# Attention kept transposed, column-tiled outputs and integer rounding in a fused attention and MLP kernel

## Chip, cores, metric

One core of one Trainium2 chip. The metric is the device time of one execution in microseconds (us), the median of several executions.

## The reference

```python
# q, k, v: (8, 8, 576, 64) float32;  g_norm: (64,)
# w_in: (512, 2048), w_out: (2048, 512): float64 (a float32 array times a NumPy scalar)
kv  = einsum('bhsd,bhse->bhde', k, v)
out = einsum('bhsd,bhde->bhse', q, kv)
rms = sqrt(mean(out * out, axis=-1, keepdims=True) + 1e-06)
x   = (out / rms * g_norm)            # -> (8*576, 8*64) = (4608, 512)
h   = x @ w_in
y   = maximum(0.01 * h, h) @ w_out    # (4608, 512) float32
```

The attention is linear: no softmax, only an RMS norm per head and token. The MLP has nine blocks of 512 tokens.

## The kernel before

A batch has 576 tokens: four tiles of 128 fill one MLP block, and the eight rests of 64 make a ninth. All matmuls are float32. TensorE turns q (transposes through PSUM), computes o token by token row, and turns the normalised x back.

```python
def load_batch(b):                       # q, k and v alike: 64 partitions in each transfer
    ...
    nc.sync.dma_start(t[:64], src[b, :, :SLO, :]...)
    nc.sync.dma_start(t[64:, :, :J], src[b, :, SLO:, :]...)

def round_f64(dst, src):                 # one tile of weights, 128 x 512
    nc.sync.dma_start(raw..., src.bitcast(U32))          # one transfer, 128 partitions
    nc.scalar.activation(low, lo, func=AF.Copy, scale=2.0 ** -52)
    nc.vector.tensor_scalar(mag, hi, 0x7FFFFFFF, None, op0=ALU.bitwise_and)
    nc.gpsimd.tensor_scalar(mag..., F64_MOST, F64_LEAST, op0=ALU.min, op1=ALU.max)
    ...                                  # three VectorE operations
    nc.gpsimd.tensor_mul(low, low, tmp.bitcast(F32))
    nc.gpsimd.tensor_add(low, low, mag.bitcast(F32))
    nc.vector.scalar_tensor_tensor(dst.bitcast(U32), in0=hi, scalar=0x80000000, in1=low..., ...)

def attend(parts):
    for h in range(H):                   # 64 columns of output a matmul
        nc.tensor.matmul(o_ps[part, h, :], lhsT=qT[:, h, :], rhs=kv[:, h, :], ...)
    ...

def mlp(b, xT, between):
    for f in range(NF + 1):              # NF = 16 chunks of 128 of the 2048
        ...                              # four matmuls into h_ps
        nc.scalar.activation(leak, h_ps, func=AF.Copy, scale=SLOPE)
        nc.vector.tensor_max(gT, h_ps, leak)
        ...                              # four matmuls of chunk f-1 into o_acc
        between(f)                       # rounding and attention steps are put here
    for t in range(4):
        nc.scalar.copy(o_sb, accs[t])    # three o_sb buffers
        store(b, t, o_sb)                # issued from ScalarE's queue

for b in range(B):
    if b == 0: go(w_steps, FC)           # twelve weight tiles before the first block
    def between(f):
        go(w_steps, 2)
        if b == 0 and f == 4: load_batch(1)
        if b > 0 or f > 7: go(a_steps, 1)
```

## Time and profile before

| | before |
|---|---|
| time, median | 1268.38 us (1267.89 to 1270.82) |
| profiled span | 1265.1 us |
| busy: TensorE / VectorE / ScalarE / GpSimd | 1203.1 / 259.5 / 223.1 / 107.3 us |
| block 0 of the MLP ends (with what comes before it: "start-up") | 243.75 us, two batches of attention done |
| later | TensorE never idle |

How to read the views: a *windows* row gives a stretch of time, its length, the busy time (and number of records) of TensorE, its weight loads, VectorE, ScalarE and GpSimd, then TensorE's granted clock, the DMA engines' share and GB/s. A *timeline* row gives start, duration, engine, source line, operation, output<-input, and in brackets the idle time before it and what ended that; a row at the edge of the window asked for is cut there, so its count can be short. "SPq" and "ACTq" are the queues that issue transfers. The rows of before stand in the prediction below. One view of before that the prediction does not show is its list of transfers (KB each, median us from issue to landing):

```profile
raw<-in_moe_w_in_dram SPq DMA_DIRECT2D x16, 512.0 KB, 3.6
```

A tile of w_in came as one transfer over 128 partitions, 3.6 us from issue to landing.

### The profile page before, as it was taken

Reading aid. Unit: us, or ns where it says so; the run is one execution under the profiler, and the core shown is the slowest. Engines: PE = TensorE matmul, PEld = TensorE weight load, DVE = VectorE, ACT = ScalarE, POOL = GpSimd, SP = SyncE. Lnnn points to the kernel's source line nnn. Section 1 sums busy time; section 2 is a strip of 40 time slices with the busy share of each in tenths; the row PEclk is TensorE's granted clock in tenths of the full one; section 3 lists DMA queues with packets and bytes.
Section 4 is the critical chain, followed back from the end, with each engine's and each line's share of the span. In section 5 each row is a group of like instructions: output and inputs, shape, how many; then the busy total and the mean of one; then the engine's idle time right before and its main releaser. Section 6 shows DMA issues by size and latency. Waiting matters only on the chain.

```text
span 1265.1 us, 9654 instructions
## 1 busy us (share of the span) xinstructions
PE 1203.1 (95%) x4048; PEld 605.6 (48%) x4048; DVE 259.5 (21%) x421; ACT 223.1 (18%) x402; POOL 107.3 (8%) x102
## 2 busy tenths in 40 slices
PE   5788579999999999999999999999999999999997
PEld 4533245465445544554455545544455444444443
DVE  0655765111001211121012100211011101011010
ACT  1411123212011310221012201220122110001001
POOL 0455654000000000000000000000000000000000
PEclk9998789999999999999999999999999999999999
DMA  8454261241014100501031101400100010001001
GB/s 181 123 153 120 96 170 47 53 75 38 0 25 83 38 1 1 100 10 37 0 71 37 38 1 34 75 1 0 34 1 1 1 30 4 1 0 34 1 0 33
DMA packets 35915, 55.14 MB, mean 44 GB/s; under 512 B 2592, under 2 KB 27168, under 8 KB 35872
## 3 DMA queue, kind: packets, MB, share of 16 engines
q1 hardware_dynamic: 29952, 45.09, 15.7%
q10 hardware_dynamic: 5920, 9.44, 3.3%
q8 instruction: 31, 0.51, 0.2%
q14 instruction: 12, 0.10, 0.0%
HBM read 45.09 MB, written 9.44 MB: 43 GB/s over the span
## 4 chain that ended last, share of the span: by engine, by line
PE 87%; DVE 5%; POOL 4%; issue 1%; DMA 1%; ACT 1%; ACTq 0%; SPq 0%; POOLq 0%; DVEq 0%
PE h_ps L252 36%; PE o_acc L265 36%; PE o_ps L183 6%; PE kv_ps L157 4%; PE q_ps L174 3%; POOL low L119 2%; POOL low L120 2%; DVE w L121 1%; DVE tmp L114 1%; PE x_ps L201 1%; POOL mag L111 1%; DMA v_in<-in_v_dram 1%; DVE mag L116 1%; DVE tmp L118 1%; DVE mag L110 1%
## 5 line engine op out<-in xcount | busy, mean ns | idle before, releaser
L265 PE MATMUL o_acc<-w,gT 128*128 128x512 f32 x1152 | 524.9, 600 | 13.7 <-DVE gT L258 13.7
L252 PE MATMUL h_ps<-xT,w 128*128 128x512 f32 x1024 | 472.4, 600 | 8.6 <-DVE w L121 7.8
L265 PEld LDWEIGHTS o_acc<-w,gT 128*128 128x128 f32 x1152 | 221.5, 193 | 296.6 <-issue 276.7
L252 PEld LDWEIGHTS h_ps<-xT,w 128*128 128x128 f32 x1024 | 189.3, 192 | 217.5 <-issue 204.7
L258 DVE TENSOR_TENSOR gT<-h_ps,leak 128x512 f32<-128x512 f32 x144 | 99.5, 691 | 692.0 <-ACT leak L256 692.0
L256 ACT ACTIVATE leak<-h_ps 128x512 f32<-128x512 f32 x144 | 85.8, 596 | 572.0 <-PE h_ps L252 572.0
L157 PE MATMUL kv_ps<-v_in,k_in 128*64 128x64 f32 (+1 forms) x640 | 60.5, 243 | 15.7 <-DMA v_in<-in_v_dram 15.7
L183 PEld LDWEIGHTS o_ps<-kv,qT 64*128 64x128 f32 x512 | 65.9, 205 | 17.8 <-issue 12.4
L183 PE MATMUL o_ps<-kv,qT 64*128 64x64 f32 x512 | 70.6, 293 | 3.2 <-DVE y L194 2.2
L157 PEld LDWEIGHTS kv_ps<-v_in,k_in 128*64 128x64 f32 (+1 forms) x640 | 50.5, 146 | 29.8 <-issue 21.0
L174 PE MATMUL q_ps<-ident,q_in 128*64 128x128 f32 (+1 forms) x320 | 49.9, 283 | 10.7 <-ACT qT L175 9.7
L252 PE MATMUL h_ps<-xT_rem,w 128*128 128x512 f32 x128 | 57.4, 592 | 0.0
L175 ACT COPY qT<-q_ps 64x512 f32<-64x512 f32 x64 | 36.9, 577 | 98.9 <-PE q_ps L174 97.1
L188 DVE TENSOR_REDUCE ss<-sq 128x8 f32<-128x512 f32 x36 | 24.7, 685 | 144.5 <-ACT sq L186 144.5
L174 PEld LDWEIGHTS q_ps<-ident,q_in 128*64 128x64 f32 (+1 forms) x320 | 30.2, 119 | 38.5 <-ACT qT L175 25.2
L119 POOL TENSOR_TENSOR low<-low,tmp 128x512 f32<-128x512 f32 x32 | 43.0, 1344 | 51.1 <-DVE tmp L118 49.5
L120 POOL TENSOR_TENSOR low<-low,mag 128x512 f32<-128x512 f32 x32 | 41.8, 1306 | 1.9
L186 ACT ACTIVATE sq<-o_ps 128x512 f32<-128x512 f32 x36 | 21.5, 597 | 113.9 <-PE o_ps L183 113.9
L252 PEld LDWEIGHTS h_ps<-xT_rem,w 128*128 128x128 f32 x128 | 24.3, 190 | 30.6 <-issue 30.6
L108 ACT ACTIVATE low<-raw 128x512 f32<-128x512 uint32 x32 | 21.7, 678 | 95.0 <-DVE w L121 84.9
L121 DVE SCALAR_TENSOR_TENSOR w<-raw,low 128x512 uint32<-128x512 uint32 x32 | 26.4, 826 | 40.2 <-POOL low L120 40.2
L202 ACT ACTIVATE xT<-x_ps,g_sb 128x512 f32<-128x512 f32 x32 | 21.2, 685 | 66.5 <-PE x_ps L201 66.5
(25 smaller groups left out, 240.3 us busy)
## 6 DMA issues: line engine op xcount, KB each, us to landing
out_dram<-o_sb ACTq DMA_DIRECT2D x72, 128.0 KB, 2.4
raw<-in_moe_w_in_dram SPq DMA_DIRECT2D x16, 512.0 KB, 3.6
raw<-in_moe_w_out_dram SPq DMA_DIRECT2D x16, 512.0 KB, 3.5
k_in<-in_k_dram SPq DMA_DIRECT2D x8, 640.0 KB, 6.1
v_in<-in_v_dram SPq DMA_DIRECT2D x8, 640.0 KB, 10.5
q_in<-in_q_dram SPq DMA_DIRECT2D x8, 640.0 KB, 6.4
k_in<-in_k_dram SPq DMA_DIRECT2D x8, 512.0 KB, 8.0
v_in<-in_v_dram SPq DMA_DIRECT2D x8, 512.0 KB, 12.3
```

The lines of the kernel that those rows point to most:

```text
L119: nc.gpsimd.tensor_mul(low, low, tmp.bitcast(F32))
L120: nc.gpsimd.tensor_add(low, low, mag.bitcast(F32))
L121: nc.vector.scalar_tensor_tensor(dst.bitcast(U32), in0=hi, scalar=0x80000000, in1=low.bitcast(U32), op0=ALU.bitwise_and, op1=ALU.bitwise_or)
L157: nc.tensor.matmul(kv_ps[:D, h, :], lhsT=k_in[:n, h, j, :], rhs=v_in[:n, h, j, :], start=(j == 0), stop=(j == JJ - 1))
L174: nc.tensor.transpose(tp[:D, h, :n], q_in[:n, h0 + h, j, :], ident[:n, :n])
L175: nc.scalar.copy(qT[:, h0:h0 + 4, :], tp[:D, :, :n])
L183: nc.tensor.matmul(o_ps[part, h, :], lhsT=qT[:, h, :], rhs=kv[:, h, :], start=True, stop=True)
L188: nc.vector.tensor_reduce(ss, sq, axis=AX.X, op=ALU.add)
L252: nc.tensor.matmul(h_ps, lhsT=w1_sb[f // FC][:, kk, (f % FC) * P:(f % FC + 1) * P], rhs=xT[:, kk, :], start=(kk == 0), stop=(kk == NK - 1))
L256: nc.scalar.activation(leak, h_ps, func=AF.Copy, scale=SLOPE)
L258: nc.vector.tensor_max(gT, h_ps, leak)
L265: nc.tensor.matmul(accs[t], lhsT=g_last[:, t * P:(t + 1) * P], rhs=w2_sb[c // FC][:, c % FC, :], start=(c == 0), stop=(c == NF - 1))
```

## The change

The intent: take transposes and narrow outputs off TensorE, and GpSimd out of the rounding.

- q is loaded in a layout that VectorE's 32x32 block transpose turns into [d, head, token]; k and v go to TensorE two heads side by side.
- o comes out transposed, [column of x, token]: for each of four groups of 128 columns of x, four matmuls of 32 weight columns each write one quarter of the PSUM partitions. x then needs no turning; the sums over a head are one matmul with a block matrix of ones.
- Tokens go straight through: block i is tokens 512i to 512i+511, so x tiles straddle batches.
- Leaky ReLU is one ScalarE pass; output copies move to VectorE.
- float64 is rounded by shifts and one integer addition on VectorE, with two ScalarE passes.

The source is not the order of the program: a scheduler in the framework orders each engine's instructions when the kernel is built. In the changed kernel it puts batch 1's attention, but for the last step, ahead of the first o_acc and batch 2's into block 0, whatever `f > 4` says.

```diff
+    def load_q(b):
+        q_in = ins.tile([P, NP, T * D], F32, tag="q_in", name="q_in", bufs=1)
+        for l in range(2):
+            for c in range(2):
+                r0, n = 64 * l + 32 * c, T * D - 32 * c
+                src = q[b].rearrange("(p l) (t s) d -> l t p (s d)", l=2, s=T)[l]
+                nc.sync.dma_start(q_in[r0:r0 + 32, :, :n], src[:, :, 32 * c:])
...
+        rows = P // len(srcs)                       # w_in: eight pieces of 16 partitions
+        for i, src in enumerate(srcs):
+            nc.sync.dma_start(raw[i * rows:(i + 1) * rows]..., src.bitcast(U32))
+        nc.scalar.activation(add, lo, func=AF.Copy, scale=2.0 ** -29)
+        nc.scalar.activation(cut, hi.bitcast(F32), func=AF.Copy, scale=2.0 ** -112)
+        nc.vector.tensor_scalar(cut, cut, HIGH_MOST, -HIGH_MOST, op0=ALU.min, op1=ALU.max)
+        nc.vector.tensor_scalar(tmp, cut.bitcast(U32), 3, None, op0=ALU.logical_shift_left)
+        nc.vector.scalar_tensor_tensor(tmp, in0=cut.bitcast(U32), scalar=0x80000000, in1=tmp,
+                                       op0=ALU.bitwise_and, op1=ALU.bitwise_or)
+        nc.vector.tensor_tensor(dst.bitcast(U32), tmp, add, op=ALU.add)
-        (the operations of before, GpSimd's three among them)
...
+        for p in range(NP):
+            nc.vector.transpose(qT[:, p, :]..., q_in[:, p, :]...)
+            for j in range(JJ):
+                for l in range(2):                  # two heads side by side
+                    nc.tensor.matmul(kv_ps[64 * l:64 * l + 64, p, :], ...)
+        if b + 1 < B:
+            load_kv(b + 1)
+            load_q(b + 1)
...
+            for e in range(NE):
+                for p in range(NP):                 # four groups of 32 columns
+                    nc.tensor.matmul(o_ps[32 * p:32 * p + 32, :], lhsT=kv[:, p, e, :, :],
+                                     rhs=qT[:, p, lo - b * S:hi - b * S], start=True, stop=True)
+            ...
+            nc.tensor.matmul(ss_ps, lhsT=same..., rhs=sq[:, 0, :], ...)
+            nc.scalar.activation(rms, ss_ps, func=AF.Sqrt, scale=1.0 / D, bias=eps_sb)
+            nc.vector.reciprocal(rms, rms)
+            nc.vector.tensor_mul(x, x, rms.unsqueeze(1).to_broadcast([P, NE, n]))
...
-                nc.scalar.activation(leak, h_ps, func=AF.Copy, scale=SLOPE)
-                nc.vector.tensor_max(gT, h_ps, leak)
+                nc.scalar.activation(gT, h_ps, func=AF.Prelu, alpha=SLOPE)
...
-            nc.scalar.copy(o_sb, accs[t])
-            store(b, t, o_sb)
+            nc.vector.tensor_copy(o_sb, accs[t])
+            nc.scalar.dma_start(out[(i * 4 + t) * P:(i * 4 + t + 1) * P, :], o_sb)
...
-        if b == 0:
-            go(w_steps, FC)
...
-            if b == 0 and f == 4:
-                load_batch(1)
-            if b > 0 or f > 7:
-                go(a_steps, 1)
+            if i > 0 or f > 4:
+                go(a_steps, 1 if i > 0 else 2)
```

## The prediction

> **What bounds the kernel now.** I read the page first (busy shares), then the windows cut where the ninth parts of the work begin, then TensorE's timeline, then the waits. The windows come first here: start-up with the first 512-token block of the MLP, then blocks 1 to 7, then block 8.
>
> ```profile
> 0.00:243.75 243.75, 188.74 (x692) 104.30 (x693) 124.21 (x206) 56.00 (x100) 107.30 (x102) 0.93 0.46 118
> 243.75:1148.09 904.34, 904.34 (x3102) 452.87 (x3100) 124.23 (x199) 154.17 (x283) 0.00 (x0) 1.00 0.13 27
> 1148.09:1266.00 117.91, 110.03 (x257) 48.45 (x255) 11.07 (x16) 12.93 (x23) 0.00 (x0) 0.98 0.07 17
> ```
>
> The columns are the window, its length, busy time of TensorE, its weight loads, VectorE, ScalarE and GpSimd, then granted clock, DMA share and GB/s. From 243.75 us on TensorE is never idle; VectorE and ScalarE are under 20% busy. So after 243.75 us only TensorE's own work counts. Before it TensorE is idle for 55 us and runs at a clock of 0.93. Some of TensorE's timeline, in and after a steady block:
>
> ```profile
> 639.76 7.03 PE L252 MATMUL h_ps<-xT,w 128*128 128x512 f32 x16
> 646.62 3.60 PE L265 MATMUL o_acc<-w,gT 128*128 128x512 f32 x8
> 650.15 6.98 PE L157 MATMUL kv_ps<-v_in,k_in 128*64 128x64 f32 x80
> ...
> 664.92 2.00 PE L183 MATMUL o_ps<-kv,qT 64*128 64x64 f32 x16
> 666.85 0.63 PE L174 MATMUL q_ps<-ident,q_in 128*64 128x128 f32 x4
> ...
> 684.41 0.60 PE L201 MATMUL x_ps<-ident,y 128*128 128x128 f32 x4
> ...
> 712.66 1.90 PE L183 MATMUL o_ps<-kv,qT_rem 64*64 64x64 f32 x32
> ...
> 773.40 7.03 PE L252 MATMUL h_ps<-xT,w 128*128 128x512 f32 x16
> ```
>
> Eight records (four float32 matmuls, two records each) start 3.43 us before what follows them, so a 128x512 float32 matmul costs 0.858 us, and a block of 128 of them 109.9 us. Blocks 1 to 7 take 904.34 us; less 7 x 109.86 that leaves 135.3 us for six batches of attention: **22.55 us of TensorE per batch**. The parts agree: kv 6.9; nine halves of o at 1.93 are 8.7; q's transposes about 4.6; x's transposes 4.5 x 0.53 = 2.4. The span is then 243.75 + 904.34 + 109.86 + 7.1 (last copies and stores) = 1265.1 us.
>
> Start-up waits for the rounding of the float64 weights. TensorE waits inside block 0, and VectorE waits for GpSimd:
>
> ```profile
> 90.61 5.40 PE L265 MATMUL o_acc<-w,gT 128*128 128x512 f32 x8 [3.64 <-DVE gT L258]
> 102.63 2.08 PE L252 MATMUL h_ps<-xT,w 128*128 128x512 f32 x2 [4.05 <-DVE w L121]
> ...
> L119 POOL TENSOR_TENSOR low<-low,tmp 128x512 f32<-128x512 f32 x32 | 43.0, 1344 | 51.1 <-DVE tmp L118 49.5
> L120 POOL TENSOR_TENSOR low<-low,mag 128x512 f32<-128x512 f32 x32 | 41.8, 1306 | 1.9
> L121 DVE SCALAR_TENSOR_TENSOR w<-raw,low 128x512 uint32<-128x512 uint32 x32 | 26.4, 826 | 40.2 <-POOL low L120 40.2
> ```
>
> Block 0 has 155 us of TensorE work in it (109.9 and two batches), and lasts 243.75: 89 us are lost to waits, cold clock and first loads.
>
> **What the Trainium skill says.** "TensorEngine Tiling (Array Packing)", Performance Considerations, gives column tiling a factor of four for 32 weight columns; "TensorE: Matmul & The Clock Gate", Part 3, measured 2.38 times for three such tiles, and says that matmuls start and end strictly in program order. No instruction of the kernel before alternates between column groups, so its trace cannot confirm it. The tiling page, Key Properties, says that a change of tiling mode drains TensorE. The trace agrees in part: each head of kv has four 128-row matmuls and one of 64 rows; a head takes 0.86 us, while ten records of qT_rem at 57 ns (1.83 / 32) would take 0.57. I read that as two changes of about 0.15 us. "ScalarE: Activation LUTs", What ACT_TABLE_LOAD costs, warns of some 2.7 us for each change of table set; the trace has two loads of 1.28 us. The order of the changed program also has two, so the leaky ReLU and the square root share a set.
>
> **The change part by part.** *TensorE per batch.* Gone: q's transposes, x's transposes, the 64-wide o. New and kept:
> - kv, 80 records of 57 ns = 4.6 us; row-mode changes halve because two heads go together. Estimate 5.0 us.
> - o: 16 matmuls of 32 weight columns over 576 tokens. At 0.858 / 512 = 1.676 ns per column that is 15.4 us one after another. Each float32 matmul is two records for the same column group, and starts keep program order, so I expect the second record of one group to run with the first of the next: half, 7.7 us. Were all four groups to run together, 3.9 us.
> - row sums: 576 x 1.676 = 1.0 us. Changes of mode around 8 visits: 1.6 us, estimated at 0.1 each.
> Sum: **15.3 us** (11.5 at full overlap, 23.1 without any), against 22.55.
>
> *MLP activation.* ScalarE's 0.60 us copy and VectorE's 0.69 us maximum become one ScalarE pass of about 0.6 us. TensorE has 6.9 us of other matmuls before it needs gT, so in steady state this is worth nothing.
>
> *Rounding.* GpSimd's 107 us vanish. Per tile VectorE keeps a clamp and a shift (0.42 each), one AND-OR (0.68) and an integer add that runs on 1,024 halves; at 1.04 ns each, read off the 0.69 us of 512, some 1.15. That is 2.7 us a tile, 86 us in 32 tiles, and ScalarE gets 1.36 us a tile. VectorE's same shift also took 1.48 us at times when GpSimd was busy, and 0.43 otherwise; that goes too. TensorE uses a tile per 3.43 us, so rounding can keep up.
>
> *Loads.* q is read twice. Its 4.6 KB runs should go as the weights' 4 KB runs do (357 to 395 GB/s at 20 to 24 us), not as k's 1.3 KB runs (about 205):
>
> ```profile
> 14.00:16.00 2.00, 0.33 (x3) 0.36 (x4) 0.00 (x0) 0.00 (x0) 0.00 (x0) 1.00 1.14 211
> ...
> 22.00:24.00 2.00, 2.00 (x17) 1.65 (x16) 0.00 (x0) 0.00 (x0) 0.00 (x0) 1.00 0.99 395
> ```
>
> A batch is then 2.36 MB at 205 plus 2.36 at 380, 18 us, hidden in a 125 us block.
>
> *Start-up.* kv of batch 0 begins at some 15 us, ends near 25; turning q (VectorE waits for kv), o, row sums and normalisation take it to about 48. In the changed order all of batch 1's attention stands ahead of the first o_acc, and batch 1's loads ahead of the fourth weight tile, so block 0 gets going at about 70 us. Then 109.9 + 15.3 (batch 2 lies in block 0) and some 15 us of stalls: the order puts several roundings on ScalarE between the ReLUs of neighbouring chunks, with only three raw buffers, about 5 us at each of three chunk changes. Block 0 ends at about **210 us**, with three batches done rather than two.
>
> *Sum.* 210 + 8 x 109.86 + 5 x 15.3 + 7 = 1172 in the profile; the timed median lies 3 us over the profiled span. **About 1174 us, 7.5% less.** Some 58 us of it is cheaper attention (8 x 7.25), the rest start-up.
>
> **The rivals.** *No overlap of column groups.* Attention is then 23.1 us a batch, as dear as before; block 0 starts at 86 and ends at 234: 234 + 879 + 115 + 10 = 1238 us. For it: nothing in this trace shows overlap, and the two float32 records per matmul may stand in its way. Against: the skill's measurement. Chance 0.3. *Full overlap*: 202 + 879 + 58 + 10 = 1149 us; chance 0.25. *Start-up stays bound.* If ScalarE's queue or eight small loads per w_in tile make rounding as slow as now, block 0 ends at 240: about 1204 with half overlap, and with no overlap about the time of before, near 1250. *VectorE becomes the bound* through turning q, the reciprocal of whole tiles and the multiplication: I count under 20 us per 125 us block, so only a record three times dearer than I think would matter.
>
> **Range and chances.** The three overlap cases give 1149, 1174 and 1238, each with some 15 us for start-up either way; so 1135 to 1240. Faster by over 2% means under 1243: sure in the two overlap cases, likely without. Chances 0.85 faster, 0.11 same, 0.04 slower.
>
> **What would show it.** Right: a steady block with attention of about 125 us; a visit of four o matmuls at 320 columns lasting some 1.1 us and not 2.1; block 0 ending near 210; GpSimd empty; TensorE without idle time afterwards. Wrong: o visits at 1.676 ns x 4 per column (no overlap); idle time of TensorE after block 0 put down to ScalarE's ReLU or to VectorE; block 0 ending at 240 with waits for w.

## The result, and the profile after

| | before | after |
|---|---|---|
| time, median | 1268.14 us | 1197.12 us (1196.87 to 1198.08) |
| ratio | 1 | 0.9444 (0.9430 to 0.9458) |
| profiled span | 1265.1 | 1195.2 |
| TensorE busy | 1203.1 | 1113.5 |
| block 0 ends | 243.75, 2 batches done | 226.76, 3 done but for 1.65 us |
| batch of attention on TensorE, steady | 22.55 us | 11.95 us |

Ratios are the mean time of one kernel's fast runs over that of the other's of the same rounds, so not quite the ratio of the medians quoted.

Windows of the kernel after: start-up, a block that begins with a pause, an undisturbed block with attention, and the last block.

```profile
0.00:226.76 226.76, 164.32 (x682) 69.86 (x683) 106.79 (x170) 69.88 (x131) 1.97 (x9) 0.89 0.69 157
338.27:465.80 127.53, 123.66 (x406) 53.14 (x404) 15.79 (x18) 16.86 (x34) 0.00 (x0) 0.99 0.21 46
849.23:971.04 121.81, 121.81 (x406) 52.48 (x405) 11.58 (x15) 16.96 (x34) 0.00 (x0) 1.00 0.03 9
1081.20:1195.20 114.00, 109.73 (x256) 48.26 (x254) 3.46 (x5) 9.55 (x16) 0.00 (x0) 0.99 0.04 16
```

An undisturbed block lasts 121.81 us; less 109.86 of MLP that is 11.95 us for a batch. The block from 338.27 lasts 5.7 us longer, of which TensorE is idle 3.87. Four of the eight blocks after start-up begin so. The last block starts at 1080.90 us, 0.3 before the last row, and holds 109.86 and a tail of 4.4 us (7.1 before). The span adds up: 226.76 + 8 x 109.86 + 1.65 + 5 x 11.95 + 23.7 (pauses) + 4.4 = 1195.1 against 1195.2.

TensorE's timeline of the kernel after, a kv visit and an o visit of four matmuls over 320 tokens with their neighbours:

```profile
481.81 0.95 PE L188 MATMUL kv_ps<-v_in,k_in 128*64 128x64 f32 x20
482.69 3.70 PE L233 MATMUL h_ps<-xT,w 128*128 128x512 f32 x8
...
554.75 3.60 PE L244 MATMUL o_acc<-w,gT 128*128 128x512 f32 x8
558.28 0.75 PE L208 MATMUL o_ps<-qT,kv 128*32 128x320 f32 x8
558.95 3.27 PE L233 MATMUL h_ps<-xT,w 128*128 128x512 f32 x7
```

The o visit lasts 0.67 us (558.28 to 558.95), where four matmuls in turn would take 4 x 320 x 1.676 ns = 2.1. Visits over 64 and 512 tokens last 0.25 and 0.99 us: 1.66 ns for each further token, the cost of *one* matmul. All four column groups run side by side. A kv visit lasts 0.88 us, four to a batch. Each visit also stretches its neighbours: eight records of o_acc start 3.53 us ahead of it, and eight of h_ps after it take 3.54 (482.69 to 486.23, where o_acc follows), against 3.43 elsewhere. So a batch is kv 3.5 + o 4 x 576 x 1.66 ns = 3.8 + 8 fixed parts of 0.14 = 1.1 + row sums 1.0 + 12 visits x 0.2 = 2.4: 11.8, near the 11.95 measured.

The pause at 600 us (VectorE, ScalarE, TensorE and the two queues, other rows left out):

```profile
587.95 1.98 SPq L90 DMA_DIRECT2D q_in<-in_q_dram  x4
...
592.62 0.69 DVE L250 COPY o_sb<-o_acc 128x512 f32<-128x512 f32 x1
...
593.35 9.61 ACTq L251 DMA_DIRECT2D out_dram<-o_sb  x4
...
601.90 0.69 DVE L250 COPY o_sb<-o_acc 128x512 f32<-128x512 f32 x1 [5.98 <-DMA out_dram<-o_sb]
603.06 1.08 ACT L237 ACTIVATE gT<-h_ps 128x512 f32<-128x512 f32 x2 [12.65 <-DMA out_dram<-o_sb]
...
603.71 6.73 PE L244 MATMUL o_acc<-w,gT 128*128 128x512 f32 x8 [3.57 <-ACT gT L237]
```

Read it upwards. TensorE waits for the ReLU; the ReLU waits in ScalarE's queue behind the fourth store; that store waits for the fourth copy; the copy waits for one of three o_sb buffers, that is for the first store to land; and the first store shares the DMA engines with the next q, whose load began 5 us earlier, when VectorE had turned the old q and so freed its single buffer. After the idle 3.57 us eight records take 6.73 us, not 3.60. That agrees with the Trainium skill, "TensorE: Matmul & The Clock Gate", Part 1, which has TensorE fall to half its clock after some 3.4 us without work. The four pauses are 3.87, 3.66, 3.57 and 3.90 us, their slow records 5.40, 5.40, 6.73 and 5.40: 15.0 + 8.5 = 23.5 us, where the four blocks are together 23.7 us longer than four undisturbed ones. Block boundaries at which no q is in flight have no pause; nor has the first one, at 226.76 us, where q's load ends about 3 us later and the fourth copy waits 3.13 us only.

Start-up of the kernel after, some of TensorE's waits:

```profile
65.91 5.55 PE L208 MATMUL o_ps<-qT,kv 128*32 128x448 f32 x16 [2.41 <-DVE qT L181]
...
86.45 3.78 PE L233 MATMUL h_ps<-xT,w 128*128 128x512 f32 x4 [6.38 <-DVE w L133]
90.69 3.84 PE L244 MATMUL o_acc<-w,gT 128*128 128x512 f32 x8 [0.46 <-ACT gT L237]
...
118.06 7.11 PE L233 MATMUL h_ps<-xT,w 128*128 128x512 f32 x12 [4.42 <-DVE w L133]
```

The first o_acc starts at 90.69 us. TensorE waits for w three times: 6.38 us, 4.42, and 4.53 at 196.38 us. The first wait is for the fourth weight tile. Its transfers are issued from 45.9 to 62.6 us, behind batch 1's loads, and its first rounding pass runs on ScalarE at 80.55 us only, behind batch 1's attention in that engine's queue. Rounding itself has become cheap (groups by form, mean ns after the comma):

```profile
L133 DVE CUSTOM_DVE_ANT_0 w<-tmp,add 128x1024 uint16<-128x1024 uint16 x32 | 22.0, 691 | 1.1
L131 DVE SCALAR_TENSOR_TENSOR tmp<-cut,tmp 128x512 uint32<-128x512 uint32 x32 | 21.8, 688 | 0.6
```

With the clamp and the shift (0.42 each) that is 2.2 us of VectorE a tile, against some 3.4 of VectorE and 3.4 of GpSimd before. How the tiles arrive has changed too (list of transfers, after):

```profile
q_in<-in_q_dram SPq DMA_DIRECT2D x16, 576.0 KB, 11.1
...
raw<-in_moe_w_in_dram SPq DMA_DIRECT2D x128, 64.0 KB, 2.5
```

A w_in tile is eight transfers now. The experiments show what that costs together with q's layout, not by itself.

### The profile page after: what moved, and what is told of

It reads as the page before. It is cut to its first block, busy times and chain, and to the rows that moved or that the text cites. A ratio compares the mean times of both kernels' runs of the same rounds, so it can differ in the third digit from the quotient of the medians.

```text
span 1195.2 us, 8362 instructions
## 1 busy us (share of the span) xinstructions
PE 1113.5 (93%) x3488; PEld 481.4 (40%) x3488; DVE 201.9 (17%) x277; ACT 184.6 (15%) x354; POOL 2.0 (0%) x9
## 4 chain that ended last, share of the span: by engine, by line
PE 81%; DMA 11%; DVE 4%; SPq 1%; ACT 1%; issue 1%; ACTq 0%; DVEq 0%
PE o_acc L244 39%; PE h_ps L233 36%; DMA q_in<-in_q_dram 5%; PE o_ps L208 3%; DMA out_dram<-o_sb 3%; PE kv_ps L188 1%; DMA raw<-in_moe_w_in_dram 1%; DVE qT L181 1%; DMA raw<-in_moe_w_out_dram 1%; SPq L121 1%; PE ss_ps L216 1%; DVE o_sb L250 1%; DVE tmp L131 1%; DMA k_in<-in_k_dram 0%; DVE w L133 0%
## 5 line engine op out<-in xcount | busy, mean ns | idle before, releaser
L233 PE MATMUL h_ps<-xT,w 128*128 128x512 f32 x1152 | 531.5, 606 | 15.7 <-DVE w L133 15.7
L233 PEld LDWEIGHTS h_ps<-xT,w 128*128 128x128 f32 x1152 | 215.7, 192 | 284.1 <-issue 260.3
L237 ACT ACTIVATE gT<-h_ps 128x512 f32<-128x512 f32 x144 | 85.5, 596 | 716.8 <-PE h_ps L233 638.7
L181 DVE STREAM_TRANSPOSE qT<-q_in 128x576 f32<-128x576 f32 x32 | 37.5, 1241 | 212.8 <-PE o_ps L208 208.4
L208 PE MATMUL o_ps<-qT,kv 128*32 128x64 f32 (+7 forms) x512 | 56.6, 463 | 13.2 <-DVE qT L181 11.3
L210 ACT ACTIVATE sq<-o_ps 128x512 f32<-128x512 f32 (+7 forms) x64 | 26.2, 410 | 203.9 <-PE o_ps L208 203.7
L188 PE MATMUL kv_ps<-v_in,k_in 128*64 128x64 f32 (+1 forms) x640 | 32.0, 243 | 17.9 <-DMA v_in<-in_v_dram 17.9
L220 DVE RECIPROCAL rms<-rms 128x512 f32<-128x512 f32 (+7 forms) x16 | 31.2, 1953 | 68.4 <-ACT rms L219 68.4
L188 PEld LDWEIGHTS kv_ps<-v_in,k_in 128*64 128x64 f32 (+1 forms) x640 | 25.7, 146 | 38.1 <-issue 35.0
L211 ACT ACTIVATE xT<-o_ps,g_sb 128x512 f32<-128x512 f32 (+7 forms) x64 | 31.6, 496 | 0.0
```

The lines of the kernel that those rows point to most:

```text
L181: nc.vector.transpose(qT[:, p, :].rearrange("p (t s) -> p s t", s=T), q_in[:, p, :].rearrange("p (s d) -> p s d", d=D)[:, :, :32])
L188: nc.tensor.matmul(kv_ps[64 * l:64 * l + 64, p, :], lhsT=k_in[:n, h, j, :], rhs=v_in[:n, h, j, :], start=(j == 0), stop=(j == JJ - 1))
L208: nc.tensor.matmul(o_ps[32 * p:32 * p + 32, :], lhsT=kv[:, p, e, :, :], rhs=qT[:, p, lo - b * S:hi - b * S], start=True, stop=True)
L210: nc.scalar.activation(sq[:, e, :], o_ps, func=AF.Square)
L211: nc.scalar.activation(x[:, e, :], o_ps, func=AF.Copy, scale=g_sb[:, e:e + 1])
L220: nc.vector.reciprocal(rms, rms)
```

## The experiments

All twelve kernels gave correct results, but for the last one.

| run | time, us | ratio to before | block 0 ends, us |
|---|---|---|---|
| after | 1197.12 | 0.9444 | 226.8 (3 batches done) |
| e1 four output buffers | 1172.05 | 0.9243 | 226.9 (3) |
| e2 kv heads apart | 1221.54 | 0.9634 | |
| e3, e4 o matmuls twice | 1216.13, 1221.11 (one run each) | | |
| e5 = e1, batch 1 later | 1165.78 | 0.9193 | 220.7 (3) |
| e6 = e5, four more tiles first | 1162.33 | 0.9166 | 215.6 (3) |
| e7 = e1, rounding of before | 1236.08 | 0.9748 | 291.9 (3) |
| e8 = before, rounding of after | 1220.68 | 0.9627 | 197.6 (2) |
| e9 = e6, weights before batches | 1152.94 | 0.9091 | 197.0 (2) |
| e10 = e9, four raw buffers | 1151.55 | 0.9079 | 194.7 (2) |
| e11 = before, ReLU of after | 1267.16 | 0.9994 | |
| e12 = after, loads over 128 partitions (wrong rows) | 1127.67 | 0.8904 | 171.7 (2) |

**The pauses: e1.** Theory A is the chain read above, buffer and store queue. The rivals leave the pauses to something else in VectorE's or ScalarE's order.

```diff
-    outp = ctx.enter_context(tc.tile_pool(name="outp", bufs=3))
+    outp = ctx.enter_context(tc.tile_pool(name="outp", bufs=4))
```

> One change to the changed kernel: four buffers for the output copies instead of three; the order of instructions on every engine is the same. Theory A (the pauses of TensorE at four block boundaries come from the fourth output copy, which waits for the first store; that store lies behind the load of the next q in the DMA engines, and ScalarE's queue holds the fourth store in front of the next block's ReLUs): the four pauses vanish with the slow clock behind them, 4 x 3.75 us of idle time and about 8.5 us of slow matmuls, so 1197 goes to about 1173 us. Rival (the ReLU is late because VectorE's copies are late behind turning q and the reciprocal, whatever the buffers): same time, 1197 us.

Measured: 1172.05 us (1171.95 to 1172.62), 25 us less. The timeline of e1 at a boundary of the same kind:

```profile
582.07 3.53 ACTq L251 DMA_DIRECT2D out_dram<-o_sb  x4
...
583.36 1.88 DVE L250 COPY o_sb<-o_acc 128x512 f32<-128x512 f32 x3
...
585.71 0.60 ACT L237 ACTIVATE gT<-h_ps 128x512 f32<-128x512 f32 x1 [6.58 <-PE h_ps L233]
...
588.70 3.60 PE L244 MATMUL o_acc<-w,gT 128*128 128x512 f32 x8
```

Three copies in one go, four stores issued in 3.53 us rather than 9.61, and o_acc without idle time although q loads at the same time. The instruction order is that of the kernel after, so the buffer was the cause.

**Column groups: e2, e3, e4.** Do two (kv) and four (o) groups really run side by side, and does a matmul that must wait for its group hold up others?

```diff
 e2:         for p in range(NP): ...
-            for j in range(JJ):
-                for l in range(2):
+            for l in range(2):
+                for j in range(JJ):
 e3:
-                for p in range(NP):
+                for p in (0, 1, 2, 3, 0, 1, 2, 3):
 e4:
+                for p in (0, 0, 1, 1, 2, 2, 3, 3):
```

> One change: k'v of the two heads of a pair one after the other, as before, and not alternating; the output still goes to the two column halves. Theory A (alternating heads overlap in the two column halves and share the changes between 128-row and 64-row matmuls): a visit of 20 records goes from 0.875 us back to about 1.7 us (6.98 / 4), 4 visits x 8 batches x 0.85 = 27 us more, 1224 us. Rival (the two column halves alone make it fast, the order does not matter): 1197 us.

> Every group of four o matmuls is done twice (same result), column groups in the order 0 1 2 3 0 1 2 3. A visit at 320 columns lasts 0.67 us in the changed kernel; one matmul takes 0.536 at 1.676 ns per column. If the four column groups run fully side by side, twice the work costs one matmul more: 1.2 us at 320 columns. If the short time of a visit is an artefact of the records, the visit would not follow: over 2 us.

> As the run before, but in the order 0 0 1 1 2 2 3 3, so that each second matmul needs the column group that the one before it holds. If each column group has a queue of its own, the visit at 320 columns takes 1.2 us as in the other order. If matmuls start strictly in program order, as the prediction supposed, the second waits for the first and holds up the other groups: five units of 0.536, about 2.7 us.

Measured: e2 1221.54 us. Its kv visit (timeline of e2):

```profile
502.03 1.80 PE L188 MATMUL kv_ps<-v_in,k_in 128*64 128x64 f32 x20
503.76 3.70 PE L233 MATMUL h_ps<-xT,w 128*128 128x512 f32 x8
```

1.73 us for the same 20 records, twice the 0.88: heads in alternation overlap in full, heads one after the other do not. Four visits x 0.85 x 8 batches = 27 us, and the time rose by 24. In e4 each column group has its four records in a row (timeline of e4):

```profile
567.32 1.30 PE L208 MATMUL o_ps<-qT,kv 128*32 128x320 f32 x16
568.55 3.70 PE L233 MATMUL h_ps<-xT,w 128*128 128x512 f32 x8
```

1.23 us in pairs, and 1.22 in turn (timeline of e3):

```profile
566.00 1.28 PE L208 MATMUL o_ps<-qT,kv 128*32 128x320 f32 x16
567.22 3.70 PE L233 MATMUL h_ps<-xT,w 128*128 128x512 f32 x8
```

A record over 320 columns costs 0.27 us, so with starts strictly in program order the pairs would need at least 13 record times (each group may start only with the last record of the one before), an estimate of 3.5 us. They need four and a little: the sixteen records of the pairs start in four rounds of four, at 567.32, 567.61, 567.88 and 568.15 us. (The built program keeps the pairs in the order of the source.) Matmuls of other groups pass a matmul that waits for its own group. An undisturbed block with attention tells the same: 125.69 us in e3 and 125.84 in e4, 3.9 and 4.0 more than in the kernel after, where 4 x 576 x 1.66 ns is 3.8. The 5 us between the two single runs lie in the pauses.

Why e2's order then gives no overlap at all stays open. Each of a head's five kv matmuls has its own weights and adds to the same output, and one of them has 64 rows, where e4's pairs repeat one matmul with the same weights; the runs do not tell these apart. The 64 rows are a strong suspect: in e2's order the 64-row matmul of one head stands between the two heads, and the starts in its trace are 0.15 us apart before and after its two records, against 0.06 between most others. If nothing runs across such a change, as the prediction quotes for a change of tiling mode, that alone would keep the heads apart.

**Start-up: what does the order of the loads cost? e5 and e6.**

```diff
 e5 (on e1):
-        if b + 1 < B:
+        if 0 < b < B - 1:
             load_kv(b + 1); load_q(b + 1)
+            if i == 0 and f == 4:        # in between(f)
+                load_kv(1); load_q(1)
 e6 (on e5), ahead of the first block:
+        if i == 0: go(w_steps, FC)
```

> The kernel with four output buffers (1172.05 us), with one thing put back as before: the loads of batch 1 (k, v, q: 4.7 MB) are issued after the fourth chunk of the first MLP block and no longer ahead of the fourth weight tile. If start-up is bound by what the loads bring and in what order, the first o_acc comes earlier than 90.7 us (the 4.7 MB take some 23 us at the 205 GB/s that they got), by 10 to 20 us, and block 0 ends near 210: 1152 to 1162 us in all. If start-up is bound by the rounding on VectorE and ScalarE, block 0 ends within 5 us of 226.9 and the time stays at 1168 to 1174. Risk: batch 1 may then come too late for block 0, with waits for it instead.

> As the run with batch 1's loads put off, and four more weight tiles are rounded before the first MLP block, as in the kernel before. Loads theory: within 5 us of that run, 1150 to 1165; the added rounding in front delays the first h_ps a little and takes away the waits for w in the first chunks. Rounding theory: no better than 1172.

Measured: the first o_acc comes at 62.60 us in e5, 28 us earlier, but the time falls by only 6: 1165.78, and 1162.33 in e6. Batch 1's attention now lies inside block 0 (12 us), and the waits have moved: e5's TensorE waits 3.44 us for q at 166 us and 4.86 for w at 190. e5 missed its range by 4 us, e6 is within its own. The order of batch 1's loads matters, but by itself it gives back little; e9 takes up the waits that are left.

**What is the rounding worth? e7, e8, e11.** e7 puts back the whole `round_f64` of before into e1 (loads as changed); e8 puts the new one into the kernel before and edits nothing else; e11 gives the kernel before the new ReLU alone.

> The kernel with four output buffers (1172.05 us), with the rounding by floating-point steps on GpSimd of the kernel before put back; everything else is as changed. If the integer rounding is what start-up gained from, block 0 ends 20 to 35 us later than 226.9, and the time is 1190 to 1207. If the loads bound start-up and rounding hides behind them, block 0 ends within 5 us of 226.9 and the time is 1170 to 1177.

> The kernel before with the rounding by integer steps alone; loads, order and attention as before. If rounding bounds its start-up (TensorE waits for VectorE, VectorE for GpSimd), block 0 ends 20 to 40 us earlier than 243.75, and the time is 1228 to 1248. If loads or the queues of ScalarE bound it too, it ends within 10 us, and the time is 1258 to 1268.

> The kernel before with the leaky ReLU as one ScalarE pass, nothing else. TensorE has 6.9 us of other work before it needs gT, so the shorter path is worth nothing: within 5 us of 1268, at most a few us less from start-up, where VectorE is freed of 0.69 us a chunk.

Measured: e7 1236.08 us, 64 more than e1, twice what I expected. Its TensorE waits for w (groups by line):

```profile
L242 PE MATMUL h_ps<-xT,w 128*128 128x512 f32 x1152 | 546.8, 619 | 53.8 <-DVE w L140 53.8
```

e8 1220.68 us: **47.5 us less than before from an edit of the rounding alone**, beyond the 20 to 40 expected. Not all else is equal, though: the scheduler kept TensorE's order, but it ordered the loads anew. Batch 2's k and v, issued at 172.8 us ahead of the last four weight tiles before, are issued at 129.4 us behind all weights in e8. The 47.5 us include what that order brings. From its page, the busy time of the engines:

```profile
PE 1189.7 (98%) x4048; PEld 602.2 (49%) x4048; DVE 224.8 (18%) x389; ACT 242.9 (20%) x434; POOL 0.7 (0%) x6
```

TensorE is busy for 98% of the span. With fast rounding and the loads of the *old* layout its timeline shows no wait for w at all; block 0 ends at 197.6 us with two batches of dear attention. The kernel after rounds as fast and has cheaper attention, and ends block 0 at 226.8, or at 216.5 with its third batch left out (11.95 less the 1.65 that lay after block 0). So its loads, their layout and their order, were the suspect. e11: 1267.16 us, no difference (0.9994, 0.9970 to 1.0018), as expected.

**Weights ahead of batches: e9, e10.** e9 is e6 with batch 2's loads moved behind the last weight loads, batch 1's one chunk earlier, and batch 1's attention begun after chunk 7; e10 adds a fourth raw buffer.

```diff
 e9 (on e6):
-        if 0 < b < B - 1:
+        if 1 < b < B - 1:
-            if i == 0 and f == 4: load_kv(1); load_q(1)
-            if i > 0 or f > 4:
+            if i == 0 and f == 3: load_kv(1); load_q(1)
+            if i == 0 and f == 11: load_kv(2); load_q(2)
+            if i > 0 or f > 7:
 e10 (on e9):
-    stage = ctx.enter_context(tc.tile_pool(name="stage", bufs=3))
+    stage = ctx.enter_context(tc.tile_pool(name="stage", bufs=4))
```

> The run with batch 1 put off and four more weight tiles in front (1162.33 us), and two more changes of order: the loads of batch 2 move behind the last weight loads (after the eleventh chunk of block 0), and batch 1's attention begins after the seventh chunk, as in the kernel before. If the waits for w at 160 and 190 us of that run (4.4 and 5.8 us) come from batch 2's loads standing ahead of weights in the one load queue, they go, and block 0 ends near 200 rather than 215: 1145 to 1155 us. If they come from the three raw buffers and ScalarE's order, the time stays at 1158 to 1164.

> The same with four raw weight buffers in place of three. If the raw buffers still hold up loads, another 3 to 8 us less than the run beside it; if not, within 2 us of it.

Measured: 1152.94 and 1151.55 us; the waits for w at 160 and 190 us are gone, and the fourth raw buffer brings 1.4 us, within the 2 that were to mean no effect. With q and w_in loaded as narrowly as before, order alone has brought the end of block 0 (two batches done) from the 216.5 of the kernel after to 197.0 us, and to 194.7 in e10. **e10 is the best correct kernel**, 9.2% under before and 3.8% under after (1151.55 / 1197.12).

**What limits a load? e12.** The prediction took q's rate from the length of its runs (4.6 KB). The Trainium skill, "SBUF — State Buffer", "Door 1: The DMA port swizzle", offers another reason: a transfer's rate goes by the ports that its partitions reach, and partitions 0 to 31 or 0 to 63 reach 8 of 16; it measured 189, 196 and 328 GB/s for 32, 64 and 128 partitions, with 218 and 436 as limits. q's four transfers cover 32 partitions each, w_in's eight 16 each.

```diff
 e12 (on the kernel after), wrong rows on purpose, the same bytes:
-        four transfers of q over 32 partitions
+        src = q[b].rearrange("h s d -> (h s d)").rearrange("(a p m) -> p a m", a=2, p=P)
+        for i in range(2):
+            nc.sync.dma_start(q_in[:, 2 * i:2 * i + 2, :], src)
-            jobs = [(w1_sb[c][:, e, :], [w_in_e[e, h, :, cols] for h in range(H)])
+            jobs = [(w1_sb[c][:, e, :], [w_in[e * P:(e + 1) * P, cols]])
```

> The changed kernel (three output buffers), wrong on purpose: each batch of q comes in two transfers over all 128 partitions (same bytes, runs of 4.6 KB as before) in place of four over 32, and each w_in tile in one transfer over 128 partitions in place of eight over 16; the rows are then the wrong ones, the amount of work the same. Partition theory (the Trainium skill's SBUF page: bandwidth goes by the ports that one transfer's partitions reach; 32 partitions reach half of them): q then loads at 330 to 400 GB/s, 6 to 7 us a batch in place of 11.5; w_in tiles land in 2 to 4 us from one issue; the boundary pauses of 3.6 to 3.9 us shrink or vanish, since stores no longer wait behind 11 us of q; block 0 ends at 190 to 210 in place of 226.8; time 1140 to 1165 us. Rival (the run length, split at 4 KB, or the reading side bounds q): q stays near 205 GB/s, the pauses stay, and only w_in's issues are saved: 1175 to 1195. The program's scheduler also puts batch 1's attention behind the first o_acc in this version, so the time of start-up is not a clean measure of the loads alone; the rates and the pauses are.

Measured: 1127.67 us, 69 less than the kernel after and below what I expected. Windows within a q load, first e12, then the kernel after:

```profile
292.00:294.00 2.00, 2.00 (x6) 0.95 (x5) 2.00 (x3) 0.00 (x0) 0.00 (x0) 1.00 1.01 417
```

```profile
464.00:466.00 2.00, 2.00 (x6) 0.95 (x5) 1.97 (x3) 0.00 (x0) 0.00 (x0) 1.00 1.03 202
```

417 GB/s against 202, at the same run length and the same full DMA share. The number of q's transfers (two for four) and the order in which they read DRAM changed too; but k and v of the same run, left over 64 partitions, load at 192 to 217 GB/s (10 to 16 us), as before. The pauses are gone with three output buffers still in place (timeline of e12):

```profile
292.68 5.32 ACTq L251 DMA_DIRECT2D out_dram<-o_sb  x4
...
296.93 0.69 DVE L250 COPY o_sb<-o_acc 128x512 f32<-128x512 f32 x1 [2.22 <-DMA out_dram<-o_sb]
298.10 0.60 ACT L237 ACTIVATE gT<-h_ps 128x512 f32<-128x512 f32 x1 [7.56 <-DMA out_dram<-o_sb]
...
300.22 2.31 PE L244 MATMUL o_acc<-w,gT 128*128 128x512 f32 x5
```

The fourth copy still waits, but 2.22 us and not 5.98, and the ReLU is done before TensorE needs it. Block 0 ends at 171.7 us with two batches done, against the 216.5 of the kernel after worked out above: some 45 us of start-up saved, and the 24 us of pauses. Two limits: the program's scheduler also put batch 1's attention behind the first o_acc here, and the two loads were changed together, so the 45 us are not split between q, w_in and order. As e9 and e10 recover 20 to 22 us of the same 45 by order alone, at most the other 23 to 25 are left for width as such. And e12 is no kernel to use: a correct layout that writes 128 partitions at once for q and for w_in was not found.

## Why the prediction was right or wrong

The direction and the range hold: 1197.12 lies in 1135 to 1240, 23 us above 1174. It is right partly by luck, by errors that cancel. In the terms of its own sum (1172 in the profile): attention after block 0 is 5 x 3.35 = 16.8 us cheaper, the pauses add 23.7, block 0 ends 16.8 later, 1.65 of batch 2 lie behind it, and the tail is 2.6 shorter; that makes the measured 1195. The range, too, is not what its text works out: with "some 15 us for start-up either way" its upper case would be 1238 + 15 = 1253, not 1240.

- **Attention, "15.3 us" a batch.** Wrong, 11.95. The failed step is "starts keep program order, so I expect ... half": the o matmuls take 3.8 us and not 7.7, all four groups side by side (e4 shows that a waiting o matmul does not hold up other groups). kv was over-estimated too (5.0, measured 3.5), the changes of mode under-estimated (1.6, measured 3.5: 0.1 a side was right, but kv's four visits and the fixed 0.14 us of each o visit were left out). Against the 22.55 of before, eight batches save 85 us, not 58. The rival "full overlap" (chance 0.25) had the right mechanism, and the wrong time, for the next reasons.
- **No idle time after block 0.** Wrong: 23.7 us in four pauses. I had counted VectorE's and ScalarE's busy time, not the queue order: stores issued by ScalarE stand ahead of the next block's ReLU, and q's single buffer starts its load just ahead of the stores. e1, with one buffer more and the same order on every engine, has none of these pauses.
- **q at 380 GB/s, 18 us a batch.** Wrong: about 205, some 23 us. Run length was the wrong measure: in e12 the same run length gives 417, over 128 partitions. I had cited 205 for k without asking why, and k's transfers cover 64 partitions.
- **Block 0 from 70 to 210 us.** Wrong: 90.7 to 226.8. The block itself lasts 136 us, near the 140 forecast, with attention in it 3.4 us cheaper; it is the start that came 21 us late. I had the order right (batch 1 ahead of the fourth weight tile and of the first o_acc) and its cost wrong: with batch 1's loads put off, the first o_acc comes at 62.6 us (e5), but the waits move and block 0 ends only 6 us earlier. Two of the "three chunk changes" stall (4.42 and 4.53 us); the 6.38 us before the first o_acc are the fourth tile's. The order of loads and steps costs some 20 us in all (e9, e10). What the narrow transfers of w_in cost, which I had seen only as a risk ("eight small loads per w_in tile"), is not measured apart from q's.
- **Rounding.** Right, and better: the integer addition on 1,024 halves takes 0.69 us, not 1.15. The 1.04 ns an element was not to be read off 0.69 us for 512, which is 1.35; the float32 products after do take 1.03 for each further element (0.692 us for 512, 1.220 for 1,024), but the add needs no more for its 1,024 halves than they do for 512. The new rounding is worth 47.5 us in the kernel before (e8).
- **Leaky ReLU worth nothing in steady state.** Right (e11).

The balance of the spans: attention 85, rounding 46 (e8's span) and a tail 3 us shorter make 134; the pauses take back 24 and start-up about 40 (the rest of the sum, not a measurement), and 70 remain. e12 gets back 69, slightly more than the 64 lost. So wide loads are enough to undo the loss, but they are not its only cause: with the loads left narrow, a fourth output buffer undoes the pauses (25 us, e1) and another order about half of the rest (e9, e10). How much of the start-up is width alone is not shown.

## What to carry to other kernels

Before a layout is changed to save compute, look at how many partitions each of its transfers writes: with 32 at a time the load rate here was half of that with 128, and what was saved on TensorE was in part spent waiting. Look at the order of the load queue in the built program as well; it gave back some 20 us without any new layout. When stores are issued from the queue of an engine that also feeds TensorE, count output buffers so that no store of a block has to wait for another, and check which load starts just before the stores. And test each part of a change by itself in the old kernel: the rounding alone, with the order of loads that came with it, gave 47.5 us there, two thirds of what the whole change gave.

## What the Trainium skill lacked or had wrong

- "TensorE: Matmul & The Clock Gate", Part 3, says that matmuls start and end strictly in program order. Column groups of float32 here do not behave so: sixteen records in pairs by group take 1.23 us over 320 columns, as in turn (1.22), where strict order would need about 3.5 (an estimate from 0.27 us a record). The kv heads of e2, one after the other, did not overlap (1.73 us for 0.88). Whether the 64-row matmul between them, and with it the drain that the prediction quotes for a change of tiling mode, makes the difference, no run here shows.
- The same part gives 2.38 times for three column tiles. Four tiles of float32 gave 2.14 (an estimate, 4 x 320 x 1.676 ns) / 0.67 = 3.2 times over 320 columns, and the cost for each further column was one matmul's (1.66 ns). No page gives the cost at the borders of a tiled visit: some 0.1 us on each side and 0.14 inside, here 3.5 us a batch.
- "SBUF — State Buffer", Door 1, agreed with what the runs showed: 202 GB/s over 32 partitions and 417 over 128 in the same 4.6 KB runs. It should be read whenever a load is re-laid.
